# Attention and maxout experts on one core: first v loads on ScalarE's queue, weight chunks one slot earlier, inversion and normalization moved within the slot

## The chip, the core and the metric

The kernel runs on one core of a Trainium2 chip. The metric is device time in microseconds, smaller is better; a kernel's time here is the median of its runs. The engines of the core are named TensorE (PE), VectorE (DVE), ScalarE (ACT), GpSimd (POOL) and SyncE (SP); SP only issues DMA transfers in this kernel.

## The reference

Soft-capped attention over 8 batches, 12 heads, 448 positions and 64 values per head, followed by a two-branch maxout layer and an output projection. In short:

```
scores = cap * tanh(q @ k.T / sqrt(64) / cap)          # cap = 30
attn   = exp(scores - max) / (sum(exp(scores - max)) + 1e-9)
x      = (attn @ v), heads put side by side            # 3584 x 768
g      = maximum(x @ w1, x @ w2)                        # 3584 x 1024
out    = g @ w_out                                      # 3584 x 768
```

## The kernel before, in words

Two heads form a head pair; there are 48 of them, six for each batch. The main loop has one **slot** for each pair `i`. Three pairs form a group `g` (16 groups), the unit of loading, casting, summing and normalizing.

The order on each engine is the order in which the Python function issues its instructions: nothing is reordered by a planner. So "slot" means a place in that order, and an instruction that waits holds everything behind it on its engine.

In slot `i`, `pv_main(i)` multiplies the exponentials of pair `i` by v (L250) and `pv_left(i)` adds the last 64 keys (L259); `pv_out(i)` copies the result to `U` (L265). Between them ScalarE computes tanh (L232, L235) and exp (L238) of pair `i+1`, and `qk` makes the scores of pairs `i+1` and `i+2` (L231, L234). The v tiles hold columns of ones beside v, so the same matmuls give the sums of the exponentials.

For a group, `gather` moves the sums into a small tile (L275); `invert` takes reciprocals on VectorE (L283), writes them to DRAM (`rec_d`, L285) and reads them back spread over the partitions (`rec_b`, L289); `normalize` multiplies `U` by them into `xT` (L305), six multiplies on POOL. `U`, `rec_b` and `xT` have two buffers each, so the u copy of group `g` has to wait for the normalize of group `g-2`.

q, k and v arrive as f32 (`load`, issued by SP at L101, L106 and L112) and are cast to bf16 by `cast` (L124, L128, L132, L137, L144), on VectorE for group 0 and on POOL for later groups. For the first 12 pairs, TensorE transposes q and k through PSUM and VectorE copies them out (`transposes`, L209 and L210). From group 4 on a DMA transpose does it (`cross`, L214), issued by SP.

The expert layer uses max(a, b) = relu(a - b) + b: `subtract` makes w1 - w2 (L168), and `turn_w2` (L175, L178) with `premultiply` (L186, L191) makes w2 @ w_out. Each goes through the six 128-row chunks of the weights. w2 and w_out come in on POOL's queue (`load_w2`, `load_wo`), w1 on SP's (`load_w1`), into two halves of the first `xT` buffer, so a chunk of w1 can only be loaded when the chunk two before it has been subtracted. Then `moe(b)` computes the layer for batch `b`: x times w1 - w2 (L318) with relu (L322), and x times w2 @ w_out plus g times w_out (L330, L333), copied to `osb` (L337) and stored (L341, L345).

These matmuls are the **fill**: they stand in a queue, and `F(n)` issues the next `n` of them at four places of each slot (8, 6, 6 and 5; fewer in the last four slots). `MS` is the slot in which the first weight chunk enters the queue. Loads and casts of coming groups stand in `todo[i]` and are issued in the middle of slot `i`. After the last slot the rest of the fill follows.

Of the kernel before, what the change touches and what calls it, by code (L numbers as in the profile page):

```python
# [10 lines left out]
def kernel(  # L11
# [11 lines left out]
    nc = tc.nc  # L23
# [11 lines left out]
    NP = H // 2  # L35
    N = B * NP
    L = 3
    G = 3
# [35 lines left out]
    def fill_const(eng, i):  # L74
        eng.memset(kf[i][:64, :, 3, 64:], 0.0)
        eng.memset(kf[i][64:, :, 3, :64], 0.0)


        eng.memset(qf[i][64:, :, 3, :], 0.0)
        eng.memset(qf[i][:64, :, 0, :], 0.0)  # L80
        for par in range(2):
            eng.memset(vp[i][:, :, par, :, 64 * (1 - par) : 64 * (2 - par)], 1.0)
            eng.memset(vl[i][64 * par : 64 * par + 64, :, 64 * (1 - par) : 64 * (2 - par)], 1.0)
# [4 lines left out]
    def half(b):  # L88
        return slice(0, 64) if b % 2 == 0 else slice(64, P)

    def load(g, what, n0=0, n1=L):
        b, p = divmod(g * L, NP)
        h0, h1 = 2 * (p + n0), 2 * (p + n1)
        src = {"k": k, "q": q, "v": v}[what]
        if (g, what) not in raw:
            raw[g, what] = (
                stage.tile([P, 2 * L, NJ * D], f32, name=what + "m"),
                stage.tile([P, 2 * L if what == "q" else L, D], f32, name=what + "l"),
            )
        m, l = raw[g, what]  # L100
        nc.sync.dma_start(  # L101
            out=m[:, 2 * n0 : 2 * n1, :],
            in_=src[b, h0:h1, 0 : NJ * P, :].rearrange("h (p j) d -> p h (j d)", j=NJ),
        )
        if what == "q":
            nc.sync.dma_start(  # L106
                out=l[half(b), 2 * n0 : 2 * n1, :],
                in_=src[b, h0:h1, NJ * P : S, :].rearrange("h p d -> p h d"),
            )
        else:  # L110
            for par in range(2):
                nc.sync.dma_start(  # L112
                    out=l[64 * par : 64 * par + 64, n0:n1, :],
                    in_=src[b, h0 + par : h1 : 2, NJ * P : S, :].rearrange("h p d -> p h d"),
                )

    def cast(eng, g, what, n0=0, n1=L):

        b = g * L // NP
        m, l = raw[g, what]  # L120
        if what == "v":
            for par in range(2):
                r = slice(64 * par, 64 * par + 64)
                eng.tensor_copy(  # L124
                    vp[g % 2][:, n0:n1, par, :, r],
                    m[:, 2 * n0 + par : 2 * n1 : 2, :].rearrange("p n (j d) -> p n j d", d=D),
                )
                eng.tensor_copy(vl[g % 2][r, n0:n1, r], l[r, n0:n1, :])  # L128
            return
        o = b % 2 if what == "q" else 0  # L130
        t = (kf if what == "k" else qf)[g % 2]
        eng.tensor_copy(  # L132
            t[:, n0:n1, o : o + NJ, :].rearrange("p n j (h d) -> p n h j d", h=2),
            m[:, 2 * n0 : 2 * n1, :].rearrange("p (n h) (j d) -> p n h j d", h=2, d=D),
        )
        if what == "q":
            eng.tensor_copy(  # L137
                t[half(b), n0:n1, 3 * (1 - o), :],
                l[half(b), 2 * n0 : 2 * n1, :].rearrange("p (n h) d -> p n (h d)", h=2),
            )  # L140
        else:
            for par in range(2):
                r = slice(64 * par, 64 * par + 64)
                eng.tensor_copy(t[r, n0:n1, 3, r], l[r, n0:n1, :])  # L144
# [11 lines left out]
    def load_wo(f):  # L156
        nc.gpsimd.dma_start(
            out=wo_sb[:, f : f + 2, :], in_=moe_w_out[f * P : (f + 2) * P, :].rearrange("(c p) n -> p c n", p=P)
        )

    def load_w2(c):
        nc.gpsimd.dma_start(out=w2b[:, c, :], in_=moe_w2[c * P : (c + 1) * P, :])
# [55 lines left out]
    def qk(i, j):  # L218

        g, n = divmod(i, L)  # L220
        t = qkT[g][:, n, :, :].rearrange("p j c -> p (j c)")
        o = Q0 + 64 * (i // NP % 2)
        qTn = t[:, o : o + S]
        if j == 0:
            tanh[i] = att.tile([P, 7, S], bf16, name="tanh", bufs=1)
            expo[i] = att.tile([P, 7, S], bf16, name="expo")
        s = s_psum.tile([P, 2, 512], f32, name="s")
        if j < NJ:
            for h in range(2):
                r = slice(64 * h, 64 * h + 64)  # L230
                nc.tensor.matmul(s[:, h, :S], t[r, j * P : (j + 1) * P], qTn[r, :])  # L231
            nc.scalar.activation(tanh[i][:, 2 * j : 2 * j + 2, :], s[:, :, :S], AF.Tanh, scale=scale / cap)  # L232
        else:
            nc.tensor.matmul(s[:, 0, :S], t[:, 3 * P : 4 * P], qTn)  # L234
            nc.scalar.activation(tanh[i][:, 6, :], s[:, 0, :S], AF.Tanh, scale=scale / cap)  # L235
# [44 lines left out]
    def invert(g, n0=0, n1=G):  # L280
        m = 16 * (n1 - n0)
        t = xpool.tile([16 * G, 56], f32, name="rec_s")
        nc.vector.reciprocal(t[:m, :], sums[g, n0][:m, :])  # L283
        d = dram.tile([16 * G, 56], f32, name="rec_d")
        nc.sync.dma_start(out=d[:m, :], in_=t[:m, :])  # L285
        rb = rec[g, n0] = xpool.tile([P, G, S], f32, name="rec_b")
        flat = d[:m, :].rearrange("(h n a) c -> h n (a c)", h=2, a=8)
        for h in range(2):
            nc.sync.dma_start(  # L289
                out=rb[64 * h : 64 * h + 64, : n1 - n0, :],  # L290
                in_=flat[h : h + 1, :, :].to_broadcast([64, n1 - n0, S]),
            )
# [56 lines left out]
    def F(n):  # L349
        while n > 0 and fill_q:  # L350
            try:
                next(fill_q[0])
                n -= 1
            except StopIteration:
                fill_q.pop(0)
# [3 lines left out]
    NT = 4  # L359
    todo = [[] for _ in range(N)]  # L360

    def at(i, f, *a):
        todo[i].append((f, a))

    for g in range(2, NL):
        e = 0 if g < NT else 2
        at(3 * g - 6 - e, load, g, "k")
        at(3 * g - 5 - e, load, g, "q")
        at(3 * g - 4, load, g, "v")
        at(3 * g - (5 if e else 4), cast, nc.gpsimd, g, "k")  # L370
        at(3 * g - (5 if e else 3), cast, nc.gpsimd, g, "q")
        at(3 * g - 2, cast, nc.gpsimd, g, "v")
        if g >= NT:
            at(3 * g - 4, cross, g)
    at(1, cast, nc.gpsimd, 1, "v")
    at(0, load_wo, 6)
    for c in range(KC):
        at(1 + c, load_w2, c)
        at(2 + c, load_w1, c)
    MS = 3  # L380

    fill_const(nc.vector, 0)
    fill_const(nc.gpsimd, 1)
    load_wo(0)
    for n0, n1 in ((0, 1), (1, L)):
        for what in "kqv":
            load(0, what, n0, n1)
    for what in "kqv":
        load(1, what)
    for what in "kq":  # L390
        cast(nc.vector, 0, what, 0, 1)
    transposes(0)
    cast(nc.vector, 0, "v", 0, 1)
    for what in "kqv":
        cast(nc.vector, 0, what, 1, L)
    qk(0, 0)
    qk(0, 1)
    ex(0, 0, 4)
    qk(0, 2)
    qk(0, 3)  # L400
    ex(0, 4, 7)
    cast(nc.gpsimd, 1, "k")
    load_wo(2)
    cast(nc.gpsimd, 1, "q")
    load_wo(4)
    transposes(1)
    qk(1, 0)
    qk(1, 1)

    for i in range(N):  # L410
        b, hp = divmod(i, NP)
        g, n = divmod(i, G)
        late = i >= N - 4
        pv_main(i)
        if i + 1 < N:
            ex(i + 1, 0, 4)
        pv_left(i)
        if i + 1 < N:
            qk(i + 1, 2)
        pv_out(i)  # L420
        if i == N - 2:
            gather(g, 0, G - 1)
        elif i == N - 1:
            gather(g, G - 1, G)
        elif n == G - 1:
            gather(g)
        if MS < i <= MS + KC:
            fill_q.append(premultiply(i - MS - 1))
        if MS <= i < MS + KC:
            fill_q.append(turn_w2(i - MS))  # L430
        if i == MS + KC:
            fill_q.append(moe(0))
        if hp == 3 and b > 1:
            fill_q.append(moe(b - 1))
        F(4 if late else 8)
        if i + 1 < N:
            qk(i + 1, 3)
            ex(i + 1, 4, 7)
        for f, a in todo[i]:
            f(*a)  # L440
        F(6)
        if i + 2 < NT * L:
            transposes(i + 2)
        F(6)
        if i == N - 1:
            invert(g, 0, G - 1)
        elif i >= G and n == 0:
            invert(g - 1)
        if i >= G and n == 1:
            normalize(g - 1)  # L450
        if i + 2 < N:
            qk(i + 2, 0)
            qk(i + 2, 1)
        F(2 if late else 5)
        if MS <= i < MS + KC:
            subtract(i - MS)
# [41 lines left out]
```

## Time and profile before

| | us |
|---|---|
| runs | 393.45, 394.06, 397.30 (median 394.06) |
| the profiled execution | 392.04 |
| its span | 390.3 |
| PE busy | 358.5 (92%) |
| ACT busy | 292.4 (75%) |
| POOL busy | 199.6 (51%) |
| DVE busy | 164.3 (42%) |

The profile is of one execution. Its page gives the busy time of each engine, the busy tenths of 40 equal slices of the span, the DMA queues, the chain of work that ended last, the costliest groups of instructions and the DMA issues. Other views of the same trace list instructions in order of time, waits with the engine that ended them, and busy time in chosen stretches. In a timeline row the columns are start, duration (both us), engine, line, operation, output<-input, shape and count; in brackets, the idle time before the row and what ended it. `SPq` is SP's queue of DMA issues. A busy PE is not PE at its peak, since matmuls are pipelined.

### The profile page before, as it was taken

To read this page: it belongs to the slowest core of one execution; us is meant where nothing else is said; L and a number is where in the kernel's file an instruction comes from. 1 tells how busy PE (TensorE), PEld (TensorE's weight loads), DVE (VectorE), ACT (ScalarE), POOL (GpSimd) and SP (SyncE) were. 2 spreads that over 40 slices of the span, in tenths; PEclk is the share of its full clock that TensorE was granted. 3 is DMA by queue.
4 is the path that set the end of the run, shared out by engine and by line. 5 is a ranking of instruction groups with operands and counts; after the bars stand their busy time and mean duration, and the time that the engine had idled before them with its cause. 6 is when DMAs were issued, how large, how long until landed. Compare 5 with 4: busy or idle time off the path is not lost.

```text
span 390.3 us, 5720 instructions
## 1 busy us (share of the span) xinstructions
PE 358.5 (92%) x2128; PEld 171.8 (44%) x2128; DVE 164.3 (42%) x248; ACT 292.4 (75%) x289; POOL 199.6 (51%) x254
## 2 busy tenths in 40 slices
PE   3468896999999999989998999999999999999995
PEld 1123443544444444434443445444444444455563
DVE  5332657774434533253325433352345333633421
ACT  2699995878899799978998899889998899400000
POOL 4272269674638374656657464729482733651000
PEclk9995998999999999999999999999999999999999
DMA  6998899786779768967989597969796751322022
GB/s 142 280 252 180 242 288 274 198 202 165 149 199 252 198 171 199 260 181 192 217 225 223 142 237 210 255 166 225 219 188 179 166 142 65 90 73 100 23 81 81
DMA packets 106596, 71.50 MB, mean 183 GB/s; under 512 B 61384, under 2 KB 99400, under 8 KB 106568
## 3 DMA queue, kind: packets, MB, share of 16 engines
q1 hardware_dynamic: 104616, 67.99, 67.6%
q0 software_dynamic: 1952, 3.15, 4.6%
q8 instruction: 16, 0.26, 0.3%
q14 instruction: 12, 0.10, 0.1%
HBM read 53.48 MB, written 11.18 MB: 166 GB/s over the span
## 4 chain that ended last, share of the span: by engine, by line
PE 54%; DMA 17%; ACT 7%; SPq 6%; POOL 6%; DVE 5%; issue 3%; POOLq 0%; DVEq 0%; ACTq 0%
PE mm L318 15%; PE mm L333 11%; PE mm L330 9%; PE pv L250 8%; DMA rec_d<-rec_s 7%; DMA rec_b<-rec_d 6%; POOL xT L305 6%; PE s L231 5%; ACT expo L238 3%; ACT tanh L232 3%; DMA vm<-in_v_dram 3%; PE pv L259 2%; SPq L112 2%; SPq L101 1%; DMA xT<-in_moe_w_dram 1%
## 5 line engine op out<-in xcount | busy, mean ns | idle before, releaser
L232 ACT ACTIVATE tanh<-s 128x896 bf16<-128x896 f32 x144 | 126.0, 909 | 36.2 <-PE s L231 35.9
L305 POOL TENSOR_TENSOR xT<-u,rec_b 64x448 bf16<-64x448 f32 x95 | 108.2, 1139 | 86.1 <-DMA rec_b<-rec_d 73.8
L238 ACT ACTIVATE expo<-tanh 128x1792 bf16<-128x1792 bf16 x96 | 144.9, 1510 | 3.0
L265 DVE COPY u<-pv 128x896 f32<-128x896 f32 x48 | 52.3, 1091 | 105.3 <-PE pv L259 80.6
L333 PE MATMUL mm<-wo_sb,gT 128*128 128x384 bf16 x448 | 88.8, 327 | 0.0
L318 PE MATMUL mm<-xT,wd_sb 128*128 128x448 bf16 x384 | 80.8, 353 | 3.3 <-POOL xT L305 1.7
L330 PE MATMUL mm<-wm_sb,xT 128*128 128x384 bf16 x336 | 68.0, 327 | 1.8 <-DVE osb L337 1.8
L250 PE MATMUL pv<-expo,vp 128*128 128x448 bf16 x288 | 66.3, 367 | 1.1 <-ACT expo L238 1.1
L333 PEld LDWEIGHTS <-gT 128*128 128x128 bf16 x448 | 41.9, 98 | 36.5 <-issue 10.8
L337 DVE COPY osb<-mm 128x384 f32<-128x384 f32 x56 | 31.0, 555 | 59.9 <-PE mm L333 54.9
L318 PEld LDWEIGHTS <-wd_sb 128*128 128x128 bf16 x384 | 35.4, 98 | 43.9 <-issue 14.5
L231 PE MATMUL s<-qkT 64*128 64x448 bf16 x288 | 46.0, 370 | 7.7 <-DVE qkT L210 5.2
L322 DVE TENSOR_SCALAR gT<-mm 128x448 bf16<-128x448 f32 x64 | 39.9, 623 | 29.6 <-PE mm L318 28.6
L330 PEld LDWEIGHTS <-xT 128*128 128x128 bf16 x336 | 31.7, 98 | 28.6 <-issue 8.7
L250 PEld LDWEIGHTS <-vp 128*128 128x128 bf16 x288 | 28.2, 101 | 29.1 <-issue 7.7
L132 POOL CAST kqf<-qm 128x1152 bf16<-128x1152 f32 x15 | 17.2, 1147 | 33.9 <-DMA qm<-in_q_dram 33.7
L235 ACT ACTIVATE tanh<-s 128x448 bf16<-128x448 f32 x48 | 26.0, 542 | 4.3 <-PE s L234 4.1
L124 POOL CAST vp<-vm 128x576 bf16<-128x576 f32 x30 | 19.9, 665 | 14.2 <-DMA vm<-in_v_dram 9.4
L132 POOL CAST kqf<-km 128x1152 bf16<-128x1152 f32 x15 | 17.2, 1147 | 12.7 <-DMA km<-in_k_dram 11.9
L231 PEld LDWEIGHTS <-qkT 64*128 64x128 bf16 x288 | 10.9, 96 | 22.8 <-issue 15.1
L209 PE MATMUL mm<-ident,kqf 128*128 128x128 bf16 x96 | 9.8, 248 | 11.5 <-DVE kqf L132 7.7
L186 PE MATMUL mm<-wo_sb,w2T 128*128 128x384 bf16 x96 | 18.7, 328 | 0.0
(44 smaller groups left out, 158.9 us busy)
## 6 DMA issues: line engine op xcount, KB each, us to landing
rec_b<-rec_d SPq DMA_DIRECT2D x30, 336.0 KB, 5.0
out_dram<-osb SPq DMA_DIRECT2D x24, 384.0 KB, 3.9
km<-in_k_dram SPq DMA_DIRECT2D x15, 576.0 KB, 7.0
qm<-in_q_dram SPq DMA_DIRECT2D x15, 576.0 KB, 4.5
vm<-in_v_dram SPq DMA_DIRECT2D x15, 576.0 KB, 4.4
xT<-in_moe_w_dram SPq DMA_DIRECT2D x6, 512.0 KB
wo_sb<-in_moe_w_out_dram POOLq DMA_DIRECT2D x4, 384.0 KB, 7.3
gT<-in_moe_w_dram POOLq DMA_DIRECT2D x6, 256.0 KB, 5.8
```

What stands on the lines that cost most here:

```text
L132: eng.tensor_copy(t[:, n0:n1, o : o + NJ, :].rearrange("p n j (h d) -> p n h j d", h=2), m[:, 2 * n0 : 2 * n1, :].rearrange("p (n h) (j d) ...
L231: nc.tensor.matmul(s[:, h, :S], t[r, j * P : (j + 1) * P], qTn[r, :])
L232: nc.scalar.activation(tanh[i][:, 2 * j : 2 * j + 2, :], s[:, :, :S], AF.Tanh, scale=scale / cap)
L238: nc.scalar.activation(expo[i][:, c0:c1, :], tanh[i][:, c0:c1, :], AF.Exp, scale=float(cap))
L250: nc.tensor.matmul(ps[:, h, :S], vp[g % 2][:, n, h, j, :], e[:, 2 * j + h, :], start=(j == 0), stop=False)
L265: nc.vector.tensor_copy(U[g][:, :, n, :], pvt[i][:, :, :S])
L305: eng.tensor_mul(xT[b // 2][r, hp, cs], U[g][r, h, n, :], rec[g, n0][r, n - n0, :])
L318: nc.tensor.matmul(ps[:, :S], wd_sb[:, c, f * P : (f + 1) * P], x[:, c, cs], start=(c == 0), stop=(c == KC - 1))
L322: nc.vector.tensor_relu(g[:, f, cs], ps[:, :S])
L330: nc.tensor.matmul(ps[:, : DM // 2], x[:, c, ts], wm_sb[:, c, hs], start=(c == 0), stop=False)
L333: nc.tensor.matmul(ps[:, : DM // 2], g[:, f, ts], wo_sb[:, f, hs], start=False, stop=(f == FC - 1))
L337: nc.vector.tensor_copy(osb[:, hs], ps[:, : DM // 2])
```

## The change

The v loads of group 0 go to ScalarE's DMA queue, ahead of its first activation. The k, q loads of groups 0 and 1 are issued ahead of the memsets in the program text. The v cast of pairs 1 and 2 moves from VectorE to POOL, and the q cast of group 1 from POOL to VectorE. The w_out chunks follow each other earlier on POOL, the first two w2 chunks come ahead of the loop and the others in slots 0 to 3, w1's chunks in slots 1 to 6, and `MS` goes from 3 to 2. Groups from 6 on have their k and q loads and casts one slot earlier. `invert` moves from the third to the first fill place of its slot. `normalize` moves from the next slot into the same slot (it was issued after `todo` of slot 3m+1, now in slot 3m), except for group 1, whose normalize is issued in slot 7 with half of its multiplies on VectorE.

```diff
-    def load(g, what, n0=0, n1=L):
+    def load(g, what, n0=0, n1=L, eng=nc.sync):
...
-        nc.sync.dma_start(
+        eng.dma_start(
...
     for g in range(2, NL):
-        e = 0 if g < NT else 2
-        at(3 * g - 6 - e, load, g, "k")
-        at(3 * g - 5 - e, load, g, "q")
+
+        t = (-6, -5, -4, -3) if g < NT else (-8, -7, -5, -5) if g < NT + 2 else (-9, -8, -6, -6)
+        at(3 * g + t[0], load, g, "k")
+        at(3 * g + t[1], load, g, "q")
         at(3 * g - 4, load, g, "v")
-        at(3 * g - (5 if e else 4), cast, nc.gpsimd, g, "k")
-        at(3 * g - (5 if e else 3), cast, nc.gpsimd, g, "q")
+        at(3 * g + t[2], cast, nc.gpsimd, g, "k")
+        at(3 * g + t[3], cast, nc.gpsimd, g, "q")
         at(3 * g - 2, cast, nc.gpsimd, g, "v")
         if g >= NT:
             at(3 * g - 4, cross, g)
-    at(1, cast, nc.gpsimd, 1, "v")
-    at(0, load_wo, 6)
     for c in range(KC):
-        at(1 + c, load_w2, c)
-        at(2 + c, load_w1, c)
-    MS = 3
-
+        if c > 1:
+            at(c - 2, load_w2, c)
+        at(1 + c, load_w1, c)
+    MS = 2
+
+    load(0, "k", 0, 1)
+    load(0, "q", 0, 1)
+    load(0, "v", 0, 1, nc.scalar)
+    load(0, "v", 1, L, nc.scalar)
+    load(0, "k", 1, L)
+    load(0, "q", 1, L)
+    for what in "kqv":
+        load(1, what)
     fill_const(nc.vector, 0)
     fill_const(nc.gpsimd, 1)
     load_wo(0)
-    for n0, n1 in ((0, 1), (1, L)):
-        for what in "kqv":
-            load(0, what, n0, n1)
-    for what in "kqv":
-        load(1, what)
     for what in "kq":
         cast(nc.vector, 0, what, 0, 1)
     transposes(0)
     cast(nc.vector, 0, "v", 0, 1)
-    for what in "kqv":
+    for what in "kq":
         cast(nc.vector, 0, what, 1, L)
+    cast(nc.gpsimd, 0, "v", 1, L)
+    load_wo(2)
...
-    cast(nc.gpsimd, 1, "k")
-    load_wo(2)
-    cast(nc.gpsimd, 1, "q")
-    load_wo(4)
     transposes(1)
     qk(1, 0)
     qk(1, 1)
+    cast(nc.gpsimd, 1, "k")
+    load_wo(4)
+    load_wo(6)
+    cast(nc.vector, 1, "q")
+    cast(nc.gpsimd, 1, "v")
+    load_w2(0)
+    load_w2(1)
...
         F(4 if late else 8)
+        if i >= G and n == 0:
+            invert(g - 1)
+        if i == NP + 1:
+            normalize(g - 1, 0, G, nc.vector)
         if i + 1 < N:
...
         if i == N - 1:
             invert(g, 0, G - 1)
-        elif i >= G and n == 0:
-            invert(g - 1)
-        if i >= G and n == 1:
+        elif i >= G and n == 0 and i != NP:
             normalize(g - 1)
```

More of the change, by code (lines that the diff above doesn't have):

```diff
@@ L105, in load @@
         if what == "q":
-            nc.sync.dma_start(
+            eng.dma_start(
                 out=l[half(b), 2 * n0 : 2 * n1, :],
@@ L111, in load @@
             for par in range(2):
-                nc.sync.dma_start(
+                eng.dma_start(
                     out=l[64 * par : 64 * par + 64, n0:n1, :],
```

## The prediction

> **What bounds the kernel now.** I read the page first, then busy time by stretch, then the timeline of single engines.
>
> ```profile
> span 390.3 us, 5720 instructions
> ...
> PE   3468896999999999989998999999999999999995
> ...
> DMA  6998899786779768967989597969796751322022
> ```
> PE is full from the eighth slice on; before that the DMA engines are. Busy time by stretch (last columns: TensorE clock, DMA share, GB/s) says so more sharply:
>
> ```profile
> 16.50:37.90 21.40, 17.36 (x83) 6.25 (x83) 5.35 (x6) 20.38 (x21) 12.31 (x20) 0.79 1.00 218
> 37.90:60.80 22.90, 19.42 (x143) 10.27 (x141) 14.06 (x18) 21.63 (x22) 11.43 (x13) 0.97 0.98 264
> ...
> 105.80:316.70 210.90, 208.09 (x1224) 97.22 (x1222) 81.91 (x119) 188.79 (x187) 121.94 (x152) 1.00 0.82 204
> ```
> So there are three regimes. Slots 1 to 4 run at ScalarE's pace, 6.08 us from one slot's second exponential (L238, 1344 wide) to the next (22.04, 28.12, 34.20). Later slots with 25 fill matmuls take 6.57 (PE), and the 48 wide L318 matmuls of a batch add 1.2. From 105.80 to 316.69 lie 31 slots: 31 x 6.57 + 5 x 1.2 - 2 x 0.49 (slots 26 and 38, whose fill runs out, fall to 6.08) = 208.7, so only **2.2 us** of the 210.9 are stalls. From 52.72 to 105.80 lie 7 slots, 7 x 6.57 + 1.2 = 47.2 of the 53.1 us, so **5.9 us** are stalls. The largest, in the timeline of ScalarE and VectorE:
>
> ```profile
> 58.73 2.10 DVE L168 TENSOR_TENSOR wd_sb<-xT,gT 128x1024 bf16<-128x1024 f32 x1 [2.97 <-DMA xT<-in_moe_w_dram]
> 59.33 1.32 ACT L238 ACTIVATE expo<-tanh 128x1344 bf16<-128x1344 bf16 x1
> ...
> 69.96 1.32 ACT L238 ACTIVATE expo<-tanh 128x1344 bf16<-128x1344 bf16 x1
> ```
> VectorE waits for the third chunk of w1; everything behind it waits too, and this interval is 10.63 us. The start, VectorE alone:
>
> ```profile
> 13.64 0.28 DVE L137 CAST kqf<-ql 64x256 bf16<-64x256 f32 x1
> 14.68 0.36 DVE L124 CAST vp<-vm 128x384 bf16<-128x384 f32 x1 [0.77 <-DMA vm<-in_v_dram]
> ...
> 15.73 0.69 DVE L210 COPY qkT<-mm 128x1024 bf16<-128x1024 bf16 x1
> ```
> The copy of the second transposes was ready when PE ended at 14.39, and stood behind four v casts. In the PE-bound part, SP and POOL:
>
> ```profile
> 204.03 3.93 SPq L214 DMA_TRANSPOSE qkT<-kqf  x1
> 208.00 0.58 SPq L101 DMA_DIRECT2D qm<-in_q_dram  x1
> ...
> 210.94 0.34 SPq L285 DMA_DIRECT2D rec_d<-rec_s  x1
> 215.41 1.12 SPq L289 DMA_DIRECT2D rec_b<-rec_d  x2
> ```
> ```profile
> 199.64 1.13 POOL L305 TENSOR_TENSOR xT<-u,rec_b 64x448 bf16<-64x448 f32 x1 [4.39 <-DMA rec_b<-rec_d]
> 200.93 5.92 POOL L305 TENSOR_TENSOR xT<-u,rec_b 64x448 bf16<-64x448 f32 x5 [0.15 <-DMA rec_b<-rec_d]
> 206.91 0.66 POOL L124 CAST vp<-vm 128x576 bf16<-128x576 f32 x1
> ```
> The inverse sums go through DRAM, the normalize waits for them, and it ends late enough to hold the u copy. From the list of waits (total, times, longest):
>
> ```profile
> DVE u L265 <- POOL xT L305: 24.7, 8, 4.5
> ...
> PE mm L209 <- DVE wm_sb L191: 3.5, 3, 3.1
> ```
> The first is mostly harmless, as the 2.2 us show; the second is where w1's wait reaches PE.
>
> **The Trainium skill.** "DMA: Bandwidth & Descriptors", section "Issuing engines are not separate DMA queues": DMAs of all engines share the same 16 DMA engines; a second issuer saves issue time only. The trace agrees as far as it goes: the share is 1.00 with POOL and SP both issuing. "TensorE: Matmul & The Clock Gate", section "Architectural detail: the array is 16× 32×32, not 1× 128×128": VectorE and ScalarE are strict FIFO; the u copy at 60.76 behind the waiting subtract shows it. "GPSIMD Engine Reference", section 1: POOL shares its SBUF interfaces with VectorE and contends with VectorE instructions of two SBUF inputs. It agrees: the subtract L168 takes 1.22 us twice with POOL idle and 2.10 to 2.19 four times with POOL busy; a POOL multiply took 1.60 instead of 1.13 beside the one VectorE multiply (0.62).
>
> **The change, part by part** (gains negative, on the profiled 392.04 us).
>
> *v on ScalarE, v casts to POOL.* Three SP issues (3.85 to 5.61, 1.76 us) leave the way of the next k, and the four v casts leave VectorE: 15.73 - 14.39 = 1.34 us. ScalarE's six issues at about 0.6 us and its 1.28 us table load end near 6, under the wait for the first scores at 8.13, so they cost nothing; without that cover 3.6 us. The first tanh of head pair 1 (17.14) cannot come before the exponential ends at 14.18, so the most is 2.96; the least is 1.34 less some 0.6 for v sharing the DMA engines with the first q, whose second load now waits for the first k to land (near 3.4, issued at 3.15 before). Loads issued ahead of the memsets change nothing: SP started at 0.75 already. I take **-2.3**, bounds -0.7 and -3.0. The q cast of group 1 now sits on VectorE (POOL: 1.15 + 0.5 us) ahead of the first u copy and waits for a load; if q lands when POOL cast it (19.57), the gain is gone. The POOL queue gains 1.5 us of casts ahead of the k cast at 17.00, which waited 11.86 us anyway.
>
> *Weights one slot earlier.* Fill starts in slot 2 and the projection of batch 0 ends in slot 13; slot 14 has no fill and takes 6.08 for 6.57: **-0.5**, both bounds near it. w2 and wo chunks are issued in a bunch on POOL, w1 chunks at slots 1 to 6; each w1 has the same distance to its subtract as before. With the DMA engines at 1.00, they cannot all come a slot earlier. Ahead of w1's third chunk the q of group 3 and k of group 4 (2 x 0.67 MB, 5 us at 264 GB/s) are gone, but the deadline is a slot (6.1 us) earlier and two w2 chunks join: I put the wait at 1.2 where PE stood 3.1 (bounds 0 and 5).
>
> *First batch on two engines.* Normalize of group 1 moves to slot 7, three multiplies on each engine. VectorE waits for the broadcast: reciprocal 1.2 us after the u copy of slot 6 starts, 0.5 to issue, 4.5 through DRAM (early groups show 5.86, 4.70, 3.68), 4.2 to land: 10.4, against 7.7 when VectorE is free. Wait 2.7, multiplies 1.9. Behind it stands the wm copy; PE fills both PSUM buffers and stops after about 3.4 us, so PE loses 2.9 (bounds 0 and 5). Together 4.1 of stall for the 5.9: **-1.8**.
>
> *Inversion forward, normalize in the same slot.* The reciprocal goes from 3.3 us after the u copy's start to 1.1 to 2.7 after. In SP's queue its DMAs pass the q load, and in slot 3 the k load and a w1 chunk, which now wait behind rec_b's wait for rec_d. Casts of k and q come a slot earlier. But on POOL **the v cast now follows the normalize**, and pv_main of the next group waits for it, at the head of PE's queue. The chain, from pv_main's start in slot 3m: SP is free after the transpose, 1.64 + 1.12 + 3.77 + 4.3 after the pv_main of the slot before, less 6.57 = 4.3; rec_d to rec_b *A*; rec_b to first multiply 4.0 (median of the pairs); six multiplies 7.35; to the second v cast less the first three pv matmuls 1.05. A is 4.2 in the mean of ten groups with the q load ahead of it (3.5 to 5.8), and 2.12 in the one group without (311.67 to 313.79). Now it follows the transpose closely: I take 2.5, so 19.2 us. Three slots take 19.2 (12, 24, 36, 42: one slot at 6.08), 19.7 (18, 30) or 20.9 (wide matmuls). Out stores stand ahead of rec_d in slots 12, 18, 30, 42 (0.6 to 1.2 each, A nearer 2.1 after two): 0.6 + 0.3 + 0.3 + 0.3 = 1.5 us of stall for the 2.2: **-0.7**, bounds -2.2 and +12.4 (below). The old hold of the u copy goes; the v cast is late next.
>
> Sum: -2.3 - 0.5 - 1.8 - 0.7 = -5.3: 392.04 becomes 386.7. The profiled execution stood 2.0 below the median of 394.06; with the same gap, **388.8**. The case's own range is 386 to 391.
>
> **Rivals.** *The v cast behind the normalize sets the pace (slower).* If A stays 4.2, the chain is 20.9, plus out stores: slots 12, 18, 24, 30, 36, 42 lose 2.3, 2.4, 1.7, 2.4, 1.7, 2.9, slots 27 and 39 lose 0.6 each: 14.6, +12.4 net, against -4.6 elsewhere: 394.06 + 7.8 = 401.9. It decides from A of about 3.3 on. For it: the transpose now lies directly ahead in the same queue. Against: the group without a q load. Chance 0.20. *The DMA engines hold the start (no change).* At share 1.00 the earlier w2 bunch only delays q of group 1 and w1; the start gain and the early gain vanish: -0.5 - 0.7, 392.9. For it: the two stretches above. Chance 0.25. *All early stalls go* (-5.9 instead of -1.8), the start gives 3.0, the late stalls 2.2: -11.6, 382.5. For it: 1.3 MB less ahead of w1. Chance 0.13. That the change doesn't do what it says is not among them: the moves stand in the changed program's instruction order.
>
> **Numbers.** Forecast 0.42. From 383.5 to 398 about a third of the slow case and half of the fast one are inside, leaving 0.19 out. About 1% (3.9 us) is what a measurement tells from no change: faster 0.51, same 0.33, slower 0.16.
>
> **What would show it.** Right: first tanh of pair 1 near 15 us; no 10 us slot, but VectorE multiplies in slot 7 waiting for rec_b; rec_d to rec_b near 2.5 us; PE's pv waiting for POOL's v cast under 2 us in all. Wrong: pv L250 waiting for POOL in each group (slow case), or the subtract still waiting for w1 by 3 us or more and the q cast holding the first u copy (no change).

## The result and the profile after

The changed kernel takes **412.15 us** (median; 409.66 to 413.65) where the kernel before took 393.77 us beside it: a ratio of **1.044, 95% interval 1.036 to 1.052**. The prediction of 388.8 us, range 383.5 to 398.0, was wrong in sign. The ratios here are taken over the fast executions of both kernels, so they are not the quotients of the medians.

The profiled execution took 409.66 us. Its page, the rows that answer to those shown of before:

```profile
span 407.9 us, 5733 instructions
...
PE   2766888399994999999999999999999998998996
...
DMA  7999697457669768888888696985784651322121
```
TensorE has two holes, a 3 in the eighth slice (71 to 82 us) and a 4 in the thirteenth (122 to 133 us), where the kernel before had none so deep after its start. In the first of them the DMA engines are at 4 tenths, so their crowding is not what holds TensorE there; in the second they are at 9, and only the waits below tell what it waited for. Busy time by stretch (columns: TensorE, its weight loads, VectorE, ScalarE, GpSimd; then TensorE clock, DMA share, GB/s):

```profile
60.80:92.00 31.20, 22.64 (x148) 11.48 (x147) 17.95 (x23) 19.55 (x20) 11.39 (x14) 0.89 0.56 150
92.00:141.00 49.00, 41.84 (x242) 18.99 (x240) 17.70 (x27) 39.04 (x39) 27.58 (x35) 0.93 0.76 189
141.00:331.00 190.00, 186.65 (x1095) 86.21 (x1092) 73.91 (x107) 169.09 (x167) 105.61 (x130) 1.00 0.77 194
```
To place the loss I took the start of the second exponential (L238, 1344 wide) of each head pair and subtracted the same pair's in the kernel before. This lag is 0.1 us at pair 4, 4.0 at pair 7, 0.0 at pair 8, **8.4** at pair 9, 9.5 at pairs 13 and 14, **13.7** at pair 16, 13.5 at pair 21, 14.7 at pair 45 and 17.5 at pair 47. Two intervals make most of it: 15.46 us between pairs 8 and 9 (slot 8), and 10.85 us between pairs 15 and 16 (slot 15). The waits of the whole execution (total, times, longest) name two causes:

```profile
PE mm L209 <- DVE wm_sb L191: 11.0, 3, 7.5
PE pv L250 <- POOL vp L124: 10.1, 10, 4.8
...
DVE wd_sb L168 <- DMA xT<-in_moe_w_dram: 7.9, 3, 5.5
```
The first interval, in the timelines of VectorE, TensorE and ScalarE (put together by time):

```profile
68.69 1.08 DVE L265 COPY u<-pv 128x896 f32<-128x896 f32 x1
69.98 1.32 ACT L238 ACTIVATE expo<-tanh 128x1344 bf16<-128x1344 bf16 x1
72.89 3.83 DVE L305 TENSOR_TENSOR xT<-u,rec_b 64x448 bf16<-64x448 f32 x3 [3.11 <-DMA rec_b<-rec_d]
76.75 0.56 DVE L191 CAST wm_sb<-mm 128x384 bf16<-128x384 f32 x1
77.36 1.01 PE L209 MATMUL mm<-ident,kqf 128*128 128x128 bf16 x8 [7.50 <-DVE wm_sb L191]
```
VectorE stands for 3.11 us at the broadcast of the inverse sums, then takes 3.83 us for three multiplies. The wm copy behind them, which frees a PSUM buffer, comes at 76.75, and TensorE has been idle since 69.86 (77.36 - 7.50). The clock that it was granted from 75.2 to 82.0 was 0.50.

The second interval, GpSimd, SyncE, VectorE and TensorE by time:

```profile
103.33 5.89 POOL L305 TENSOR_TENSOR xT<-u,rec_b 64x448 bf16<-64x448 f32 x5 [1.17 <-DMA rec_b<-rec_d]
109.29 0.66 POOL L124 CAST vp<-vm 128x576 bf16<-128x576 f32 x1
111.27 1.30 PE L250 MATMUL pv<-expo,vp 128*128 128x448 bf16 x6
113.23 1.15 POOL L132 CAST kqf<-qm 128x1152 bf16<-128x1152 f32 x1
114.64 0.48 DVE L283 RECIPROCAL rec_s<-sums 48x56 f32<-48x56 f32 x1
114.85 3.72 SPq L214 DMA_TRANSPOSE qkT<-kqf  x1
117.89 0.51 POOL L137 CAST kqf<-ql 64x384 bf16<-64x384 f32 x1
119.30 0.38 SPq L285 DMA_DIRECT2D rec_d<-rec_s  x1
121.51 1.13 SPq L289 DMA_DIRECT2D rec_b<-rec_d  x2
126.80 5.87 POOL L305 TENSOR_TENSOR xT<-u,rec_b 64x448 bf16<-64x448 f32 x5 [0.29 <-DMA rec_b<-rec_d]
132.70 4.77 SPq L214 DMA_TRANSPOSE qkT<-kqf  x1
132.73 0.67 POOL L124 CAST vp<-vm 128x576 bf16<-128x576 f32 x1
133.45 2.42 PE L250 MATMUL pv<-expo,vp 128*128 128x448 bf16 x6 [4.78 <-POOL vp L124]
```
Read it as a chain. GpSimd ends a normalize at 109.22; the casts of v, then of k and q of group 5, follow. SyncE's transpose waits for those casts until 114.85 and occupies SyncE's queue to 118.57. The reciprocal started at 114.64, yet its DMA stands behind the transpose and an out store and leaves at 119.30. So the next normalize ends at 132.67, the next v cast comes after it, and TensorE has waited for it for 4.78 us. The next transpose, at 132.70, is no longer part of this: it is group 6's, whose casts had ended at 118.40, since the change has them one slot earlier from group 6 on.

### The profile page after: what moved, and what is told of

It is laid out like the page before. It is cut to its first block, busy times and chain, and to the rows that moved or that the text cites. A ratio compares the mean times of both kernels' runs of the same rounds, so it can differ in the third digit from the quotient of the medians.

```text
span 407.9 us, 5733 instructions
## 1 busy us (share of the span) xinstructions
PE 360.5 (88%) x2128; PEld 171.3 (42%) x2128; DVE 166.9 (41%) x249; ACT 293.0 (72%) x289; POOL 196.7 (48%) x253
## 4 chain that ended last, share of the span: by engine, by line
PE 45%; DMA 25%; POOL 15%; DVE 6%; issue 4%; SPq 4%; POOLq 0%; DVEq 0%
PE mm L318 14%; POOL xT L305 10%; PE mm L333 9%; DMA rec_b<-rec_d 8%; DMA rec_d<-rec_s 7%; PE pv L250 7%; PE mm L330 7%; DMA xT<-in_moe_w_dram 5%; PE s L231 3%; PE pv L259 2%; DMA km<-in_k_dram 2%; DMA qm<-in_q_dram 2%; POOL vp L124 2%; DVE u L265 1%; SPq L289 1%
## 5 line engine op out<-in xcount | busy, mean ns | idle before, releaser
L305 POOL TENSOR_TENSOR xT<-u,rec_b 64x448 bf16<-64x448 f32 x92 | 105.6, 1149 | 148.6 <-DMA rec_b<-rec_d 118.0
L238 ACT ACTIVATE expo<-tanh 128x1792 bf16<-128x1792 bf16 x96 | 145.0, 1510 | 3.0
L250 PE MATMUL pv<-expo,vp 128*128 128x448 bf16 x288 | 68.2, 372 | 10.7 <-POOL vp L124 10.1
L124 POOL CAST vp<-vm 128x576 bf16<-128x576 f32 (+1 forms) x32 | 21.3, 665 | 5.7 <-DMA vm<-in_v_dram 4.9
```

The lines of the kernel that those rows point to most:

```text
L238: nc.scalar.activation(expo[i][:, c0:c1, :], tanh[i][:, c0:c1, :], AF.Exp, scale=float(cap))
L250: nc.tensor.matmul(ps[:, h, :S], vp[g % 2][:, n, h, j, :], e[:, 2 * j + h, :], start=(j == 0), stop=False)
L305: eng.tensor_mul(xT[b // 2][r, hp, cs], U[g][r, h, n, :], rec[g, n0][r, n - n0, :])
```

## The experiments

Two theories came from these traces. **S**: VectorE's wait and multiplies of group 1 (the third step) hold TensorE. **L**: the normalize ahead of the v cast (the fourth step) closes a loop through GpSimd's and SyncE's queues, from the casts of k and q by way of the transpose and the inverse sums to the next normalize. In the expectations of the first four runs L has only its simple form V, "the v cast stands behind a normalize". Rival **D** was that the crowded DMA engines hold the start, whoever works on what. All ratios are to the kernel before, run on the same chip beside each; its median lay between 394.2 and 395.5 us.

### Group 1 on GpSimd alone

```diff
         if i == NP + 1:
-            normalize(g - 1, 0, G, nc.vector)
+            normalize(g - 1)
```


> Kernel after, with one change: in slot 7 all six multiplies of group 1 run on GpSimd, none on VectorE. Theory S (VectorE's wait for rec_b in slot 7 and its three 1.27 us multiplies hold the wm copy L191, and so TensorE for 7.5 us and ScalarE for 9.0): the 15.46 us slot falls to 8 or 9, L209 waits under 2 us for L191, and the time falls by 5 to 8 us, to 404 to 407. Rival D (the crowded DMA engines hold slots 1 to 8 whoever multiplies): slot 8 is shorter but a wait for w1 or for the broadcast turns up one slot on, and the time stays within 2 us of 412. Theory V (the v cast behind the normalize is the main loss): 410 to 412, and slot 15 is long as before.

Measured: **412.06 us, ratio 1.044 (1.040 to 1.049)**: nothing gained. This is V's number, but V alone does not explain it: the interval before pair 9 did fall as S says, from 15.46 to 6.61 us, and the lag at pair 9 is 0.2 us. A new interval, 13.17 us before pair 13, takes the gain back; the lag there is 8.8. GpSimd, SyncE and TensorE by time:

```profile
73.31 6.91 POOL L305 TENSOR_TENSOR xT<-u,rec_b 64x448 bf16<-64x448 f32 x5 [0.24 <-DMA rec_b<-rec_d]
80.28 0.66 POOL L124 CAST vp<-vm 128x576 bf16<-128x576 f32 x1
84.21 1.15 POOL L132 CAST kqf<-qm 128x1152 bf16<-128x1152 f32 x1
85.83 3.79 SPq L214 DMA_TRANSPOSE qkT<-kqf  x1
91.02 0.55 SPq L285 DMA_DIRECT2D rec_d<-rec_s  x1
101.31 5.87 POOL L305 TENSOR_TENSOR xT<-u,rec_b 64x448 bf16<-64x448 f32 x5 [0.31 <-DMA rec_b<-rec_d]
107.24 0.66 POOL L124 CAST vp<-vm 128x576 bf16<-128x576 f32 x1
107.96 2.42 PE L250 MATMUL pv<-expo,vp 128*128 128x448 bf16 x6 [3.82 <-POOL vp L124]
```
The multiplies taken off VectorE keep GpSimd to 80.22 instead of 75.23. The k and q casts end at 85.80 and SyncE's transpose starts with that; a q load (1.3 us) and then the inverse sums follow it, and one group later TensorE waits for the v cast. No expectation named this: the stall is S's, but curing it feeds another one.

### Normalize behind the v cast

```diff
-        elif i >= G and n == 0 and i != NP:
+        if i >= G and n == 1 and i != NP + 1:
             normalize(g - 1)
```


> Kernel after, with one change: the normalize of every group but group 1 goes back to the slot after the inversion (3m+1), so that GpSimd does the v cast before it; the inversion stays half a slot forward. Theory V (TensorE's pv waits for a v cast that stands behind a normalize, in slots 15, 30, 33, 45): slot 15 falls from 10.85 to about 6.6 us, pv L250 no longer waits for the v cast, and the time falls by 5 to 8 us, to 404 to 407. Theory S alone: falls by 1 us at most, to 411. Rival D: no change in the first 100 us, so at most the 5 us that lie behind slot 14.

Measured: **401.74 us, ratio 1.019 (1.014 to 1.024)**. TensorE no longer waits for the v cast anywhere. The interval before pair 16 is 6.78 us, and behind it the lag falls from 12.3 to 8.6 us. The interval before pair 9 stays, at 16.31 us (TensorE's wait for the wm copy: 8.1 us). About 10 us gained, more than expected.

### Both

The two edits together.

> Kernel after with both changes: group 1's six multiplies on GpSimd, and every other normalize back behind the v cast. If S and V are separate losses, their savings add: 398 to 401 us. What is then left over the kernel before (about 4 to 7 us) belongs to the start and to the weights one slot earlier. If it lands at or below 394, these two parts cost nothing; if it stays above 404, rival D holds most of the loss.

Measured: **392.98 us, ratio 0.996 (0.993 to 0.999)**, 5 us or more better than expected: nothing of the loss stays. The four kernels make a square of ratios:

| normalize of other groups | group 1 on two engines | group 1 on GpSimd |
|---|---|---|
| ahead of the v cast | 1.044 | 1.044 |
| behind the v cast | 1.019 | 0.996 |

The two losses do not add. VectorE's part costs 2.3% where GpSimd has slack, and nothing where GpSimd's delay would be paid for anyway.

### The start alone

Before, with `load(0, "v", ...)` on `nc.scalar`, all loads ahead of the fills, and `cast(nc.gpsimd, 0, "v", 1, L)`.

> Kernel before with the start of the change alone: v loads of group 0 issued by ScalarE, loads ahead of the constant fills, v casts of head pairs 1 and 2 on GpSimd; weights, inversion and normalize as before. By the prediction's first step: the first tanh of pair 1 comes 2.3 us earlier and the time falls by 1 to 2.5 us, to 391.5 to 393. Rival (the first scores themselves come later, because v now shares the DMA engines with the first q, and the second exponential of pair 0 is 1.6 us late as in the kernel after): the same or up to 1.5 us slower, 394 to 395.5.

Measured: **394.62 us, ratio 0.998 (0.995 to 1.0005)**, not told from no change. The second load of the first q is cast at 10.73 us here, 9.59 in the kernel with both repairs, 7.77 in the kernel after, 6.19 before. In the six profiled executions with this start it came at 7.77 to 11.13 us, in the eight with the old one at 5.82 to 6.27. The lag at pair 1 is +1.4 us in this execution.

```profile
7.62 0.36 DVE L132 CAST kqf<-qm 128x384 bf16<-128x384 f32 x1 [0.97 <-DMA qm<-in_q_dram]
10.73 0.22 DVE L137 CAST kqf<-ql 64x128 bf16<-64x128 f32 x1 [2.75 <-DMA ql<-in_q_dram]
```

### The fourth step alone

```diff
         F(4 if late else 8)
+        if i >= G and n == 0:
+            invert(g - 1)
...
         elif i >= G and n == 0:
-            invert(g - 1)
-        if i >= G and n == 1:
             normalize(g - 1)
```
and the table of loads and casts of the change.

> Kernel before with the fourth step alone: inversion half a slot forward, normalize of every group in the same slot (six multiplies on GpSimd, ahead of the next v cast), casts and loads of k and q one slot earlier; start, weights and first batch as before. Theory L (a loop through two queues: normalize, then v cast, then casts of k and q on GpSimd; SyncE's transpose waits for those casts; the inverse sums stand behind the transpose; the next normalize waits for them; a delay of GpSimd comes back a group later and reaches TensorE at the v cast): 8 to 16 us slower than before, 403 to 411, with TensorE's pv waiting 3 us or more for the v cast in at least two groups. The prediction's fourth step (a chain that starts at TensorE in each group and has no memory of GpSimd's delay): 393 to 395.

Measured: **410.49 us, ratio 1.037 (1.030 to 1.044)**, +14.5 us: this one step is nearly the whole loss. Its lag is 1.5 us at pair 8, 6.4 at pair 9, 13.3 at pair 13 and 18.5 at pair 47. The waits of TensorE for the v cast, and of SyncE's transpose for GpSimd's casts:

```profile
PE pv L250 <- POOL vp L124: 11.3, 15, 3.8
...
SPq L214 <- POOL kqf L137: 26.1, 5, 11.7
```
The longest of the first are 3.76 and 1.73 us; I had expected two above 3. Not all of the 13.3 us is the loop: the 12.03 us interval before pair 9 has TensorE waiting 3.8 us for a wm copy behind a subtract that waits 4.5 us for w1, while in this execution rec_d took 7.7 us to rec_b with the DMA share at 0.85. The loop shows at groups 4 and 5: their transposes start at 91.41 and 117.61, within 0.05 us of the end of their q casts; that of group 6 starts at 134.81, over 13 us after its own.

### The weights alone

```diff
-    at(0, load_wo, 6)
     for c in range(KC):
-        at(1 + c, load_w2, c)
-        at(2 + c, load_w1, c)
-    MS = 3
+        if c > 1:
+            at(c - 2, load_w2, c)
+        at(1 + c, load_w1, c)
+    MS = 2
```
with the last wo and the first two w2 chunks issued before the loop.

> Kernel before with the second step alone: w2 and w1 chunks, their turning, premultiply and subtract one slot earlier; all else as before. If the DMA engines bring w1's third chunk at the same time whatever the slot that asks for it: the 10.6 us slot comes one slot earlier and the total is 393 to 396, no difference. If earlier issue helps (the prediction's early part): 391 to 393. If the weights crowd out k and q in the first five slots: 396 to 399.

Measured: **398.23 us, ratio 1.006 (1.004 to 1.009)**, 2.5 us slower. Intervals before pairs 3, 4 and 5 are 7.1, 8.4 and 7.8 us, where before had 6.08: a q cast of GpSimd waits 7.1 us for its load, and the first subtract waits 5.6 us for w1. This q was issued at 21.46, ahead of w1 (23.02), so it was not behind it in a queue; the DMA share from 16.5 to 37.9 was 1.11, against 1.00 before.

```profile
37.21 1.15 POOL L132 CAST kqf<-qm 128x1152 bf16<-128x1152 f32 x1 [7.08 <-DMA qm<-in_q_dram]
42.44 1.23 DVE L168 TENSOR_TENSOR wd_sb<-xT,gT 128x1024 bf16<-128x1024 f32 x1 [5.56 <-DMA xT<-in_moe_w_dram]
```

### Both repairs with the old start

Group 0's loads again by SyncE in the order k, q, v; `cast(nc.gpsimd, 1, "q")`; the v cast of pairs 1 and 2 stays on GpSimd.

> The kernel with both repairs (group 1 multiplied on GpSimd, every other normalize behind the v cast), and the start put back: group 0's v loads by SyncE behind k and q as in the kernel before, q cast of group 1 on GpSimd; only the v cast of pairs 1 and 2 stays on GpSimd. If the v loads on ScalarE delay the first q (its second load was cast at 7.8 to 10.7 us with them, 6.2 without): the first scores come 1.5 to 3.5 us earlier than in the kernel with both repairs, the second pair's exponential 0.5 to 2 us earlier, total 391 to 392.5. If the start is of no account because w1's third chunk holds slot 6 or 7 anyway: 393, as without.

Measured: **393.76 us, ratio 0.997 (0.994 to 1.0003)**. The start is better (second exponential of pair 1 at 20.93 us, against 22.34 in the kernel with both repairs and 22.04 before; 20.83 to 23.88 in the six executions with the start of the change), and it is given back at once: the intervals before pairs 5 and 7 are 9.2 and 9.6 us, and VectorE waits 9.1 us in all for w1. The second expectation held.

### One link of the loop cut

```diff
-            at(3 * g - 4, cross, g)
+            at(3 * g - 3, cross, g)
```
in the kernel after.

> Kernel after with one link of the loop cut: SyncE's transpose of group g is issued in slot 3g-3, behind the inverse sums of that slot instead of ahead of them. The slot 8 of 15.5 us stays. Theory L: rec_d is issued within 1 us of the reciprocal (4.7 us in slot 15 of the kernel after), the waits of pv for the v cast (10.1 us in all) fall below 4, and the time falls by 5 to 8 us, to 404 to 407. Rival (the normalize of 7.3 us ahead of the v cast is too long in itself, whatever SyncE does): less than 2 us, 410 to 412. Rival (the transpose is now late and qk waits for it): slower than 412.

Measured: **425.16 us, ratio 1.073 (1.066 to 1.081)**. The last rival came true, but the trace also shows the link. SyncE and TensorE:

```profile
116.62 0.35 SPq L285 DMA_DIRECT2D rec_d<-rec_s  x1
118.03 1.12 SPq L289 DMA_DIRECT2D rec_b<-rec_d  x2
119.25 4.92 SPq L214 DMA_TRANSPOSE qkT<-kqf  x1
...
170.29 0.93 PE L231 MATMUL s<-qkT 64*128 64x448 bf16 x4 [3.28 <-DMA qkT<-kqf]
```
rec_d leaves 0.5 us after the reciprocal (116.11) instead of 4.7, and TensorE's waits for the v cast are gone, from 10.1 us to none. In their place the scores wait 19.3 us in ten places for the transposes. That is not a clean cut, since these new stalls also give GpSimd time; but it shows that the inverse sums of that slot were late because of the transpose ahead of them.

### The early groups repaired alone

```diff
-        elif i >= G and n == 0:
+        elif i >= G and n == 0 and g > 5:
             normalize(g - 1)
+        if i >= G and n == 1 and g <= 5:
+            normalize(g - 1)
```
in the kernel with the fourth step alone.

> The kernel with the fourth step alone (410.5 us), but the normalizes of groups 0 to 4 stand behind the v cast as in the kernel before, those of groups 5 to 15 ahead of it. Theory L (GpSimd is late after the first batch, when it also casts and issues weights, and the loop hands this delay on; later groups lose 1 us each at most): the 13 us lost before slot 13 disappear, 396 to 400. The prediction's slow rival (each group loses 1.7 to 2.9 us, most of them after slot 15): 405 to 409.

Measured: **397.67 us, ratio 1.013 (1.007 to 1.020)**: theory L's range, and 2.3% below the kernel with all normalizes ahead (1.0133 / 1.0368). The lag at pair 13 is 1.8 us instead of 13.3. So some 9 of the 14.5 us lie with the early groups. The other 5 stay: TensorE still waits for the v cast, 1.4 us at the longest but 6.1 in all, and the lag grows to 4.8 us at pair 47.

### The inversion forward with the v cast first, and two additions

The first kernel is the fourth step alone with `normalize(g - 1)` left at `n == 1`. The second adds the v cast of pairs 1 and 2 on GpSimd. The third adds this:

```diff
+    for c in range(KC):
+        at(1 + c, load_w2, c)
+        at(2 + c, load_w1, c)
     for g in range(2, NL):
...
-    for c in range(KC):
-        at(1 + c, load_w2, c)
-        at(2 + c, load_w1, c)
```
so that in each slot the weight chunks are issued ahead of the k and q loads, and w2's on GpSimd also ahead of its casts.

> Kernel before with the inversion half a slot forward and the casts and loads of k and q one slot earlier, but the normalize where it was, behind the v cast; start, weights and first batch as before. Theory L: the whole loss of the fourth step comes from the normalize standing ahead of the v cast, so this kernel has none of it and keeps what the kernel with both repairs gained after slot 12 (its lag over the kernel before fell from +2.5 us to -1.5 us): 390 to 392.5. Rival (the earlier inverse sums or casts cost something themselves, behind SyncE's transpose): 395 or more.

Measured: **393.66 us, ratio 0.999 (0.996 to 1.002)**. The 14.5 us of the fourth step are gone, all of them due to the place of the normalize; the gain that I had expected is not to be seen. This kernel and the one of the last section differ only in the later groups' normalizes: ahead of the v cast they cost 1.4% (1.013 against 0.999).

> The kernel with the inversion forward and the v cast first, and in addition the v cast of head pairs 1 and 2 on GpSimd instead of VectorE, with the loads on SyncE in the order of the kernel before. In the kernel with both repairs and the old start, this brought the second pair's exponential 1.1 us earlier. If that reaches the end: 389.5 to 391.5, about 1 us below the kernel without it. If w1's third chunk takes it back in slot 7: the same within 0.5 us.

Measured: **391.65 us, ratio 0.9965 (0.993 to 0.9998)**. This is just above the range expected. The subtract waits 9.2 us for w1 in five places.

> The kernel with the inversion forward, the v cast first and the v cast of pairs 1 and 2 on GpSimd, and in addition each w1 chunk issued ahead of the k and q loads of its slot instead of behind them (w2 chunks keep their slots). What is left of early stall there: the subtract waits 9.2 us in all for w1, slots 6 to 9 take 7.1 to 8.6 us instead of 6.6, and the second exponential of pair 14 is 1.5 us behind the kernel before. If w1 is late because k and q loads stand in front of it: the waits halve and the time falls by 1 to 3 us, to 389 to 391. If the DMA engines are simply full in that stretch: k and q come later instead, the k or q cast holds the transposes, and the time is the same within 1 us or worse.

Measured: **388.29 us, ratio 0.982 (0.978 to 0.987)**: faster than both kernels of this case, by 1.8% than the one before and by 5.9% than the one after (0.9825 / 1.0439 = 0.941). The waits for w1:

```profile
DVE wd_sb L168 <- DMA xT<-in_moe_w_dram: 5.4, 2, 3.8
```
In the profiled execution, the slowest of its six at 391.04 us, one of them still costs a 12.68 us interval before pair 10: that w1 chunk is issued at 68.19, behind a broadcast of the inverse sums that waits from 60.99 to 67.01 for rec_d. Up to pair 47 this execution stands 1.1 us behind that of the second kernel, so the trace does not show where the 1.4% come from; what the other executions have was not seen.

## Why the prediction was wrong

**Step 4, the inversion and the normalize, is the step that failed.** It forecast -0.7 us; alone it costs 14.5 (11.7 to 17.4). The chain had the right members and four of its five durations were right. In the group of the 10.85 us interval, from pv_main of pair 12 at 111.27: rec_d to rec_b 2.21 (2.5 assumed), to the first multiply 3.86 (4.0), the multiplies 7.29 (7.35), to the end of the wait 0.79 (1.05). The first term, **"SP is free after the transpose ... 4.3"** behind pv_main, measured 8.03 (0.6 of it an out store, which the forecast counted apart). I had fixed the transpose to TensorE's clock, as it stood in the kernel before. But it waits for GpSimd's k and q casts, which had now moved behind a normalize that itself waits for SyncE. The sum is 22.2 us, TensorE came for v after 17.4 (19.2 assumed), and the difference is the 4.78 us wait. So for these groups the chain has a memory: it must be added up around the loop, and a group that starts late passes it on. The loop is closed for groups 4 and 5 only. From group 6 on, the change casts k and q one slot earlier, ahead of that slot's normalize, and the transpose finds them ready. The waits for v fit this. In the kernel after, in the one with group 1 on GpSimd and in the one with the fourth step alone, all that last 3.5 us or more lie in slots 12 and 15, which use the v of groups 4 and 5; the others are of 2.0 us at most. The kernel with only the early groups repaired has 2.3% back for five of sixteen groups. No kernel here moves those casts alone, so this reason for the early place of the loss is read from traces, not tested.

**The slow rival** named the right wait, and had 0.20. Its rule, "it decides from A of about 3.3 on", did not cover the longest wait: A was 2.2 in that group (it was 4.2 and 3.9 before the smaller waits of slots 30 and 33). Its size, 14.6 us spread over slots 12 to 42, came near by luck, since the early stalls hold much of it. But a part is spread as it says: from slot 18 on the kernel after has 5.3 us of waits for v (10.1 - 4.78), where the forecast had put 1.5 for all slots, and the later normalizes cost 1.4%.

**Step 3, the first batch on two engines** (-1.8). Three terms were off. VectorE's wait was 3.1 us for 2.7. Its three multiplies took 3.83 us for 1.9: I had taken 0.62 each from the one multiply of the kernel before, beside which GpSimd's took 1.60 instead of 1.13. "GPSIMD Engine Reference", section 1 of the Trainium skill says that the two engines contend when a VectorE instruction has two SBUF inputs; I had drawn that on GpSimd's side only. Here both pay: VectorE's three took 1.36, 1.55 and 1.08 us, and of GpSimd's instructions beside them one multiply took 1.50, and a v cast 1.05 instead of 0.66. And TensorE's cover was nil: it had stopped at 69.86, when VectorE began to wait, so it lost 7.5 us and not 2.9, outside the bound of 5, and the clock that it then had until 82.0 was 0.50. The stall is real (2.3% once GpSimd has slack), yet it is worth nothing in the kernel after, as the square shows.

**Step 1, the start** (-2.3). The v casts off VectorE did bring the second copy of transposes 1.2 us forward in the kernel after (14.51 for 15.73, against 1.34), though not with the start alone (15.88). The charge for v sharing the DMA engines with the first q, 0.6 us, was the mis-sized term: that q was 1.6 to 4.9 us later than before in the six executions with this start. The sign that I had named, the first tanh of pair 1 near 15 us, was there (15.92, before 17.14), and proved nothing for the end. The cover that I had warned of also failed, in the kernel after (VectorE):

```profile
19.55 1.35 DVE L132 CAST kqf<-qm 128x1152 bf16<-128x1152 f32 x1 [4.35 <-DMA qm<-in_q_dram]
21.28 1.07 DVE L265 COPY u<-pv 128x896 f32<-128x896 f32 x1
```
The first u copy was at 20.29 before. Alone, the start is worth nothing that can be told.

**Step 2, the weights** (-0.5). Alone +2.5 us (1.4 to 3.6). The forecast looked only at what stands ahead of w1; the other side, q beside w1 and w2 on full DMA engines, is where 7.1 us of wait went. The rival that the DMA engines hold the start had this part right.

The three steps alone sum to about +16 us (-0.8 + 2.5 + 14.5), close to the 17.3 of the whole. The square warns against reading more into that: parts that share a queue need not add.

**Where the inversion's own gain went.** With every normalize behind the v cast, the inversion half a slot forward gains 3.7 us after pair 16 (lag +2.2 to -1.5 with both repairs), and 3.8 us as a kernel of its own (3.9 to 0.1). But that kernel had lost 4 us before. In slot 3 the inverse sums now stand ahead of w1's second chunk. SyncE before, then with the inversion forward, and VectorE's subtract there:

```profile
39.55 0.64 SPq L165 DMA_DIRECT2D xT<-in_moe_w_dram  x1
...
38.82 0.35 SPq L285 DMA_DIRECT2D rec_d<-rec_s  x1
43.15 1.11 SPq L289 DMA_DIRECT2D rec_b<-rec_d  x2
46.45 0.60 SPq L165 DMA_DIRECT2D xT<-in_moe_w_dram  x1
53.86 2.13 DVE L168 TENSOR_TENSOR wd_sb<-xT,gT 128x1024 bf16<-128x1024 f32 x1 [4.74 <-DMA xT<-in_moe_w_dram]
```
The chunk leaves 6.9 us later, because the broadcast ahead of it waits until 43.15 for rec_d; the interval before pair 7 is 12.42 us, and the lag grows from 0.1 us at pair 6 to 3.4 at pair 9. The prediction had named this order and put no cost on it. The second of the three kernels and the one with the early groups repaired issue the chunk equally late (45.91 and 46.01).

**What stays open.** From the second exponential of pair 47 to the end takes 55.0 us in the kernel before and 58.0 in the profiled execution with the inversion forward alone: TensorE waits 3.2 us instead of 1.8 for work behind the last multiply of VectorE, and the clock granted from 354.4 to 357.8 is 0.50. The profiled executions of the start alone (58.2) and of the second of the three kernels (58.3) have this end too; how often it comes was not settled. Nor was what the 1.8% of the fastest kernel is made of.

## What to carry to other kernels

When an instruction is moved ahead of another on an in-order engine, follow the instruction that is now behind to its consumer, and on through every queue until the path either ends or comes back to the moved one; if it comes back, add the whole loop and ask what delay enters it, not only what each group needs. A stall on one engine may be the slack of another: test two suspects together as well as one by one, since curing either may show nothing. And in a stretch where the DMA engines are full, the order of issue within a slot (0.9825 against 0.9965 in the last two kernels) can be worth more than the slot; here that rests on the times alone.

## What the runs showed of the hardware

- VectorE's multiply of two SBUF operands (64x448, f32 to bf16) took 0.62 us in the kernel before, while the GpSimd multiply beside it took 1.60 instead of 1.13. In slot 7 of the kernel after, three of VectorE's took 1.36, 1.55 and 1.08 us beside GpSimd's multiplies and casts. Either side can pay.
- After TensorE's long waits for v the next six pv matmuls took 2.42 us instead of 1.30 (after 4.78, 3.82 and 3.76 us, and once after 1.96), so such a stall costs at least 1.1 us beyond its length. In the kernel after, the clock granted from 129.8 to 136.6, around the end of the longest of them, was 0.50. In the kernel with the early groups repaired, whose waits for v are at most 1.4 us, it was 1.00 from 76 to 395.
- The DMA transpose held SyncE's queue for 3.7 to 4.8 us in the kernel after, and 4.9 to 6.1 us where it was issued directly behind the broadcast of the inverse sums.
